# An attention kernel's second pair of heads: spread by transfers, rotated in one piece, with products of zeros behind two score chunks

## The chip, the cores and the metric

The kernel runs on one core of one Trainium2 chip. The metric is the device time of one execution in microseconds (us). Engines are named as the profile names them: PE (TensorE, matrix products and transposes), PEld (its weight loads), DVE (VectorE), ACT (ScalarE), POOL (GpSimd), and SP, the queue from which most transfers are issued.

## The reference

The program is an attention layer followed by two feed-forward layers, in float32. Attention has 4 batches of 8 heads, 576 positions and 64 columns per head:

```python
q_rot, k_rot = (rotate(q), rotate(k))     # rotary embedding, cos/sin by position
scores = scale * np.matmul(q_rot, k_rot.transpose(0, 1, 3, 2))
scores = scores - np.max(scores, axis=-1, keepdims=True)
attn = np.exp(scores)
attn = attn / (np.sum(attn, axis=-1, keepdims=True) + 1e-09)
return np.matmul(attn, v).astype(np.float32)
```

Its result, 2304 tokens of 512 columns, goes through `g = s * relu(x @ w_in)**2 + b; g @ w_out` (2048 hidden columns), and then through `silu(x @ w_gate) * (x @ w_val) @ w_out` with `silu` on the first factor (1536 hidden columns).

## The kernel before, in words

**Order of work.** The kernel is written as a list of operations (`op`, `sch.dma`), each with an engine, an estimated duration, a priority (lower goes first), dependences, and tokens for the buffers that it takes and gives back. A planner (`Schedule.run`, L63) plays the list through with these estimates: whenever an engine is free it takes the ready operation of lowest priority number that finds its buffers free, and emits its instructions. So the order on each engine and on the SP queue is fixed when the program is built. Only dependences of data are waited for on the chip. `o.next.append(x); x.need += 1` orders x behind the planned end of o without a wait on data. An operation that depends on one of its own engine becomes ready 0.06 us after the other's planned end; in that gap the planner gives the engine to whatever else is ready.

**Attention** works on 16 pairs of heads (two heads side by side in the 128 partitions). `prep(p)` (L448) loads a pair's queries and keys into `x` (two buffers), rotates them into `ry` (two buffers) in four steps, transposes `ry` on PE in three groups (L549, into the three PSUM banks `t`), and then spreads the transposed values, split into a high part and a rest for float32r products, into three arrays: `a` (queries, high and rest), `t` (keys, rest and high) and `kz` (keys, high, and zeros in the other rows). There are two sets of these, for even and odd pairs (z = 0, 1).

- Pair 0 rotates on DVE in three pieces. Pairs 1 and later rotate on POOL, each step one instruction over the whole pair: `y0` (L518), `y1` (L520), `y2` (L523), `y3` (L526). Pair 1 begins with a copy (L517) that waits for pair 0's rotation.
- Pairs 0 and 1 are spread by ACT and DVE (the `else` branch, L564 to L581): for each of three groups ACT writes `t`'s high part (L566), `a`'s high part (L566) and a copy of the first into `kz` (L568), and DVE writes the two rests (L571). Half of `kz` (64 partitions) was zeroed by POOL at the start (`zero`, L397).
- Pairs 2 and later: the layout of `ry` puts query and key columns alternately (L484), ACT writes one high part of all 128 rows into `qkhi` per group (`hi`, L556), DVE one rest into `qklo` (`lo`, L558), and five transfers on SP (`sp`, L586 to L598) copy every second row into `a`, `t` and `kz`. POOL zeroes `kz` whole ahead of that for pairs 2 and 3 (L585).

A pair's **values** are split on POOL in two instructions per head: `v0` (L611) and `v1` (L613), in `vh`.

`pair(p)` (L629) does nine score chunks of 128 queries (`s_mm`, L661, two PSUM buffers `s`), for each of them the row maximum on DVE (L664) and the exponential with its sum on ACT (L668). A chunk's PSUM buffer is free for the next chunk but one after its exponential. Of every three chunks, a `third` (L708) transposes the exponentials on PE (L724, L727), splits them on ACT (`ph`, L732) and DVE (`pl`, L739), multiplies them by the values (L754, L756) into the one bank `v`, and copies the result out on ACT (L767).

At the start PE runs 60 small products of zeros (`warm`, L435, L442) in the `v` bank.

```python
for i in range(WARM):
    op("pe", 0.11, warm, -100, (zeros[0][0],), (warm_tok,) if i == 0 else (), (warm_tok,))
```

The priorities that matter here: pair 0's and pair 1's `prep` have -390 and -290, pair 2's -40, pair 3's 60; pair 0's chunks run from 0 to 81, pair 1's from 100; the values of pair p, head j have 100p + 20j; the loads of values have 100p - 60 (pair 0 and 1: -200 and 40).

The feed-forward layers follow. Their weights are loaded and converted during the second half of attention, tied to score chunks of certain numbers.

Of the kernel before, what the change touches and what calls it, by code (L numbers as in the profile page):

```python
# [8 lines left out]
F32 = mybir.dt.float32  # L9
# [155 lines left out]
def t_pool(n):  # L165
    return 2.35e-3 * n + 0.08
# [11 lines left out]
def tile_attention_moe_moe(  # L178
# [34 lines left out]
    NE = 7  # L213
    LATE, LAST = 1 << 20, 1 << 21
    WARM = 60
    TP = 100
    PREP = 240
    TA = 50
# [178 lines left out]
    def zero(z, prio):  # L397
        o0 = op("pool", 0.2, lambda: nc.gpsimd.memset(a_t[z][:, S:S + 64].bitcast(F32), 0.0), prio)
        for x in (hi_t[z], lo_t[z]):
            gaps.append(op("pool", 0.2, lambda x=x: nc.gpsimd.memset(x[:, S:S + 64].bitcast(F32), 0.0), -250))  # L400
        o1 = op("pool", 1.0, lambda: nc.gpsimd.memset(kz_t[z][64:128].bitcast(F32), 0.0), prio)
        return (o0, o1)

    def load_x(p, g0, g1, prio, st, x_tok, after=()):
# [36 lines left out]
    for i in range(WARM):  # L441
        op("pe", 0.11, warm, -100, (zeros[0][0],), (warm_tok,) if i == 0 else (), (warm_tok,))  # L442

    first_rope = []

    qk_ops = list(sch.ops)

    def prep(p):  # L448
# [32 lines left out]

        def take_ry():
            st["ryt"] = rp_p.tile([128, PC, 2 * D], F32, tag="ry", name="ry")
            st["ry"] = st["ryt"].rearrange("p c (a d j) -> p j c a d" if p > 1 else "p c (j a d) -> p j c a d", j=2, a=2)  # L484

        def views2(a):
            return st["x"].rearrange("p j c (a d) -> p j c a d", a=2)[:, :, :, a], st["ry"][:, :, :, a]
# [4 lines left out]
        for g in range(G):  # L492
# [20 lines left out]
            if o is None and p:  # L513
                def y0():
                    take_ry()
                    if p == 1:
                        nc.gpsimd.tensor_copy(st["ryt"][:, 0, 0:1], first_rope[1]["ryt"][:, PC - 1, 2 * D - 1:2 * D])  # L517
                    nc.gpsimd.tensor_tensor(out=views2(0)[1], in0=views2(1)[0], in1=table(3, 1, 0, PC), op=ALU.mult)  # L518
                def y1():
                    nc.gpsimd.tensor_tensor(out=views2(1)[1], in0=views2(0)[0], in1=table(2, 1, 0, PC), op=ALU.mult)  # L520
                def y2():
                    xv = st["x"]
                    nc.gpsimd.tensor_tensor(out=xv, in0=xv, in1=table(0, 2, 0, PC), op=ALU.mult)  # L523
                def y3():
                    rv = st["ry"].rearrange("p j c a d -> p j c (a d)")
                    nc.gpsimd.tensor_tensor(out=rv, in0=st["x"], in1=rv, op=ALU.add)  # L526
                n2 = PC * D
                for y, fn in enumerate((y0, y1, y2, y3)):
                    o = op("pool", t_pool(n2 if y < 2 else 2 * n2), fn, pr, (o, *lds[0], *rt_op, *first_rope[:1]), (ry_tok,) if y == 0 else (), (x_tok,) if y == 3 else ())
                st["rope"] = o  # L530
            elif not p:
              o = None
              for y, fn in enumerate((r1, r0, r2, r3)):
                last = o if y else st.get("roped")
                deps = [*lds[g], (rt_ld[g], rt_op[2 * g], rt_op[2 * g + 1], None)[y]]
                o = op(eng, tt(fd if y > 1 else fd // 2), fn, pr + g, deps, (ry_tok,) if y == 0 and g == 0 else (),
                       (x_tok,) if y == 3 else (), port=eng == "dve")
                if last is not None:
                    last.next.append(o)
                    o.need += 1  # L540
              st["roped"] = o
              if g == G - 1:
                  first_rope.append(o)
                  first_rope.append(st)
# [3 lines left out]
                for c in range(PC // G):  # L548
                    nc.tensor.transpose(taken(ps)[:, :, c * 64:(c + 1) * 64], st["ryt"][:, g * (PC // G) + c], ident.rearrange("p (h r) -> p h r", h=2))  # L549
            hi_x, lo_x = hi_t[z], lo_t[z]  # L550
            acq = (ps_tok, hi_tok if p > 1 else tok) if g == 0 else (ps_tok,)
            prt = pr + 3 + g
            o = st["tr"] = op("pe", 0.33, tr, prt, (o, eye_op, st.get("tr"), *(zeros[z] if p < 2 else ())), acq, (ry_tok,))
            if p > 1:
                def hi(g=g):
                    nc.scalar.activation(out=place(hi_x, g), in_=taken(st["ps", g]), func=AF.Copy, scale=qs_t)  # L556
                def lo(g=g):
                    nc.vector.scalar_tensor_tensor(  # L558
                        out=place(lo_x, g), in0=taken(st["ps", g]), scalar=qs_t, in1=place(hi_x, g).bitcast(F32), op0=ALU.mult, op1=ALU.subtract
                    )  # L560
                o = st["hi0"] = op("act", t_act(CG, True, 1), hi, prt, (o, eye_op, st.get("hi0")))
                trs.append(op("dve", t_dve(CG, 2), lo, prt, (o,), (), (ps_tok,)))
            else:
                def act(dst, rows, g=g):  # L564
                    scale = D ** -0.5 if rows is up else 1.0
                    return lambda: nc.scalar.activation(out=place(dst, g), in_=taken(st["ps", g])[rows], func=AF.Copy, scale=scale)  # L566
                def again(dst, src, g=g):
                    return lambda: nc.scalar.activation(out=place(dst, g), in_=place(src, g).bitcast(F32), func=AF.Copy)  # L568
                def sub(dst, src, rows, g=g):
                    scale = D ** -0.5 if rows is up else 1.0  # L570
                    return lambda: nc.vector.scalar_tensor_tensor(  # L571
                        out=place(dst, g), in0=taken(st["ps", g])[rows], scalar=scale, in1=place(src, g).bitcast(F32), op0=ALU.mult, op1=ALU.subtract
                    )
                o1 = op("act", t_act(CG), act(t[dn], dn), prt, (o,))
                o2 = op("act", t_act(CG), act(a[up], up), prt, (o,))
                later = g if p == 0 else 0
                ops += [o1, op("dve", t_dve(CG), sub(t[up], t[dn], dn), prt, (o1,), (), (ps_tok,)),
                        op("act", t_act(CG, False), again(kz[up], t[dn]), prt, (o1,))]
                st.setdefault("a", []).append([o2, op("dve", t_dve(CG), sub(a[dn], a[up], up), prt + 3 * later, (o2,), (), (ps_tok,))])
                if p or g == 0:  # L580
                    ops += st["a"][-1]  # L581
        if p > 1:
            cleared = ()
            if p < 4:
                cleared = (op("pool", t_pool1(SP), lambda: nc.gpsimd.memset(kz.bitcast(F32), 0.0), pr + 6, trs[:1], (tok,)),)  # L585
            def sp(o, i, first=False):  # L586
                return sch.dma(
                    256 * SP, lambda: nc.sync.dma_start(out=o.bitcast(F32), in_=i.bitcast(F32)), pr + 6, (*trs, *cleared, *gaps),
                    (tok,) if first else (), (hi_tok,), pace=1.1
                )  # L590
            ev, od = slice(0, 128, 2), slice(1, 128, 2)
            ops = [
                sp(a[ev], hi_x[ev], p > 3),
                sp(a[od], lo_x[ev]),
                sp(t[ev], lo_x[od]),
                sp(t[od], hi_x[od]),
                sp(kz[ev], hi_x[od]),
            ]  # L598
            for o in ops[1:]:
                ops[0].next.append(o)  # L600
                o.need += 1
# [4 lines left out]
        for j in range(2):  # L606
            def part(j, h):
                return st["vh"][j][:, :, D * h:D * h + D]
            def v0(j=j):
                st["vh"][j] = v_p.tile([128, 5, 2 * D], F32R, tag="vh", name="vh")  # L610
                nc.gpsimd.tensor_scalar(out=part(j, 0), in0=st["vr"][:, j], scalar1=1.0, scalar2=0.0, op0=ALU.mult, op1=ALU.add)  # L611
            def v1(j=j):
                nc.gpsimd.tensor_tensor(out=part(j, 1), in0=st["vr"][:, j], in1=part(j, 0).bitcast(F32), op=ALU.subtract)  # L613
            vt = st["vh_tok"][j] = Token("vh")
            o = op("pool", t_pool1(320), v0, base + 20 * j, vls, (vt,))
            st["vh_op"][j] = op("pool", t_pool(320), v1, base + 20 * j, (o,), (), (tok_v,))
        return st

    turns, s_turns, v_turns = [], [], []

    def in_turn(o, turns=turns):
        if turns:
            turns[-1].next.append(o)
            o.need += 1
        turns.append(o)
# [3 lines left out]
    def pair(p, st):  # L629
# [10 lines left out]
        for u in range(NU):  # L640
# [32 lines left out]
                main = [*main, *st["a"][1 + u // 2]]  # L673
            o = s_prev = op("pe", t_mm(HS, 4 * len(terms)), s_mm, pr, (*main, s_prev), (s_tok, l_tok, *((sums[b]["tok"],) if pp == 0 else ())) if u == 0 else (s_tok,), (opb,))
            in_turn(o, s_turns)
            o = op("dve", t_dve(S), mx, pr, (o,))
            exps[u] = op("act", t_act(S, True, 1) + 0.09, ex, pr + 1, (o,), (e_tok[u],), (s_tok, l_tok))

# [280 lines left out]
        p, tag = (ps_t, "t") if tok.pool == "t" else (ps_v, "v")  # L959
        return p.tile([128, 512], F32, tag=tag, name="hb")[:, 0:n]  # L960

    sts, ends = {}, []
    for p in range(NP):
        sts[p] = prep(p)
    for p in range(NP):
        ends += pair(p, sts[p])
    n_att = len(sch.ops)
# [699 lines left out]
```

## Time and profile before

| | |
|---|---|
| median of 3 runs | 1093.91 us (1093.45 to 1094.46) |
| profiled execution | 1094.09 us, its span 1092.3 us |
| busy over the span | PE 1076.9, PEld 973.7, DVE 891.9, ACT 737.4, POOL 203.7 us |
| attention's score chunks | from 12.5 to 285 us |
| granted PE clock | 1.00 over the span |

The span is cut from the first to the last instruction of the profiled execution; the time of the execution is 1.8 us longer. Busy time is that of instructions at work; waits for semaphores and issuing of transfers don't count. A timeline row has the start, the duration and the operation; in brackets stands the idle time of the engine ahead of it, and what ended it.

### The profile page before, as it was taken

What the parts mean: (1) busy time and instruction counts of PE and PEld (TensorE: products, weight loads), DVE (VectorE), ACT (ScalarE), POOL (GpSimd) and SP (SyncE); (2) the same over time, 40 slices, a digit from 0 to 9 for tenths busy, and PEclk for the clock granted to TensorE, in tenths of its full rate; (3) what the DMA queues carried; (4) which work ended last, traced back from release to release, by engine and by line L of the source; (5) the groups of instructions that cost most, each with busy time, mean ns of one, the idle gap of its engine ahead of it and who ended that gap; (6) DMA issues with size and microseconds to landing.
All of it is one profiled execution on the core that took longest, in us unless ns stands there. A gap on an engine that the chain in (4) does not pass through costs nothing.

```text
span 1092.3 us, 17578 instructions
## 1 busy us (share of the span) xinstructions
PE 1076.9 (99%) x6188; PEld 973.7 (89%) x6188; DVE 891.9 (82%) x1575; ACT 737.4 (68%) x1511; POOL 203.7 (19%) x167
## 2 busy tenths in 40 slices
PE   8999999999999999999999999999999999999998
PEld 7899988888888799999888888999989999899996
DVE  6999999999988998879999998876596675976751
ACT  6998999999887776656665556655565554655550
POOL 7998878622210000000000000000000000000000
PEclk9999999999999999999999999999999999999999
DMA  4666867565569554482456654312231122311102
GB/s 124 205 201 218 272 215 246 144 227 181 141 221 259 156 173 164 141 237 87 167 184 204 227 173 140 132 56 70 88 96 39 58 68 78 96 50 44 54 1 57
DMA packets 111192, 155.51 MB, mean 142 GB/s; under 512 B 34416, under 2 KB 67200, under 8 KB 111104
## 3 DMA queue, kind: packets, MB, share of 16 engines
q1 hardware_dynamic: 110288, 153.60, 45.1%
q8 instruction: 49, 0.80, 0.3%
q10 hardware_dynamic: 816, 0.79, 0.2%
q14 instruction: 39, 0.32, 0.1%
HBM read 99.98 MB, written 32.58 MB: 121 GB/s over the span
## 4 chain that ended last, share of the span: by engine, by line
PE 81%; DVE 10%; ACT 4%; DMA 2%; issue 2%; POOL 1%; SPq 0%; DVEq 0%; POOLq 0%; ACTq 0%
PE hb L858 14%; PE hb L860 14%; PE hb L859 14%; PE acc L859 5%; PE acc L860 5%; PE acc L858 5%; PE acc L1449 5%; PE acc L1450 5%; PE acc L1448 5%; PE ps_s L661 3%; DVE nm L664 3%; DVE pl L739 3%; PE ps_t L724 2%; PE ps_av L754 2%; PE ps_av L756 1%
## 5 line engine op out<-in xcount | busy, mean ns | idle before, releaser
L858 PE MATMUL hb<-w 128*128 128x384 f32 (+1 forms) x728 | 250.9, 345 | 0.0
L860 PE MATMUL hb<-w 128*128 128x384 f32 (+1 forms) x728 | 250.5, 344 | 0.0
L859 PE MATMUL hb<-w 128*128 128x384 f32 (+1 forms) x728 | 250.1, 344 | 0.0
L858 PEld LDWEIGHTS hb<-w 128*128 128x128 f32 x728 | 136.7, 188 | 9.1 <-ACT tmp L1251 0.6
L859 PEld LDWEIGHTS hb<-w 128*128 128x128 f32 x728 | 136.7, 188 | 7.4
L860 PEld LDWEIGHTS hb<-w 128*128 128x128 f32 x728 | 136.6, 188 | 4.6
L668 ACT ACTIVATE e<-ps_s,nm 128x576 f32<-128x576 f32 x144 | 107.1, 744 | 9.9 <-DVE nm L664 8.9
L732 ACT ACTIVATE ph<-ps_t 128x512 fp32r<-128x512 f32 x192 | 105.7, 569 | 10.4 <-PE ps_t L724 9.2
L664 DVE TENSOR_REDUCE nm<-ps_s 128x1 f32<-128x576 f32 x144 | 107.8, 751 | 5.4 <-PE ps_s L661 4.2
L859 PE MATMUL acc<-gl,w 128*128 128x512 f32 (+1 forms) x288 | 107.0, 371 | 0.6 <-DVE gl L919 0.6
L860 PE MATMUL acc<-gh,w 128*128 128x512 f32 (+1 forms) x288 | 106.8, 371 | 0.0
L858 PE MATMUL acc<-gh,w 128*128 128x512 f32 (+1 forms) x288 | 106.6, 370 | 0.0
L661 PE MATMUL ps_s<-t,a 128*128 128x288 f32 x320 | 99.9, 329 | 4.6 <-ACT e L668 4.5
L739 DVE TENSOR_TENSOR pl<-ps_t,ph 128x512 fp32r<-128x512 f32 x144 | 95.4, 683 | 3.2 <-ACT ph L732 2.5
L754 PE MATMUL ps_av<-ph,vh 128*128 128x384 f32 (+1 forms) x320 | 97.0, 331 | 0.6 <-DVE ph L739 0.5
L1509 ACT ACTIVATE tmp<-hb 128x384 f32<-128x384 f32 x144 | 70.4, 489 | 34.3 <-PE hb L860 32.8
L661 PE MATMUL ps_s<-kz,a 128*128 128x288 f32 x320 | 88.9, 294 | 0.0
L724 PE MATMUL ps_t<-ident,e 128*128 128x128 f32 x576 | 86.1, 274 | 1.9 <-DVE a L571 1.1
L724 PEld LDWEIGHTS ps_t<-ident,e 128*128 128x128 f32 x576 | 67.8, 140 | 10.3 <-issue 1.7
L1147 DVE TENSOR_TENSOR w<-sums,w 128x512 fp32r<-128x512 f32 x104 | 68.3, 686 | 7.7 <-ACT w L1145 7.5
L756 PE MATMUL ps_av<-pl,vh 128*64 128x384 f32 (+1 forms) x256 | 72.5, 295 | 0.0
L661 PEld LDWEIGHTS ps_s<-t,a 128*128 128x128 f32 x320 | 60.2, 188 | 10.4 <-ACT e L668 9.1
(136 smaller groups left out, 2415.8 us busy)
## 6 DMA issues: line engine op xcount, KB each, us to landing
raw<-gv SPq DMA_DIRECT2D x36, 512.0 KB, 3.7
raw<-in_moe_w_out_dram SPq DMA_DIRECT2D x28, 512.0 KB, 4.0
x_d<-xr SPq DMA_DIRECT2D x64, 144.0 KB, 2.9
raw<-in_moe_w_in_dram SPq DMA_DIRECT2D x16, 512.0 KB, 3.8
raw<-up SPq DMA_DIRECT2D x16, 512.0 KB, 5.3
raw<-in_moe_w_gate_dram SPq DMA_DIRECT2D x12, 512.0 KB, 4.5
raw<-in_moe_w_val_dram SPq DMA_DIRECT2D x12, 512.0 KB, 4.8
gv<-dec SPq DMA_DIRECT2D x24, 256.0 KB, 2.5
```

What stands on the lines that cost most here:

```text
L661: nc.tensor.matmul(ps[:, hf * 512:hf * 512 + HS], a[:, q0:q0 + 128], m[:, k0:k0 + HS], start=y == 0, stop=y == len(todo) - 1)
L664: nc.vector.tensor_reduce(out=st["nm"][:, u:u + 1], in_=st["s", u], axis=AX.XY, op=ALU.max, negate=True)
L668: nc.scalar.activation(out=st["e", u].rearrange("p (f n) -> p f n", f=2), in_=st["s", u], func=AF.Exp, bias=st["nm"][:, u:u + 1], accum_ou ...
L724: nc.tensor.transpose(ps[:, z * 128:z * 128 + 128], st["e", u][:, kc * 128:kc * 128 + 128], ident)
L732: nc.scalar.activation(out=st["ph", y][0:rows, 512 * i:512 * i + n], in_=st["pt", y, i][0:rows, 0:n], func=AF.Copy)
L739: nc.vector.tensor_tensor(out=dst, in0=st["pt", y, i][0:rows, 0:n], in1=st["ph", y][0:rows, c].bitcast(F32), op=ALU.subtract)
L754: nc.tensor.matmul(ps, vv, st["ph", y][:, c], start=kc == 0, stop=kc == 4, skip_group_check=True)
L756: nc.tensor.matmul(ps[0:64], vv[:, 0:64], st["pl", y][:, c], start=False, stop=False, skip_group_check=True)
L858: nc.tensor.matmul(o, lh, rh, start=first, stop=False, skip_group_check=more)
L859: nc.tensor.matmul(o, lh, rl, start=False, stop=False, skip_group_check=more)
L860: nc.tensor.matmul(o, ll, rh, start=False, stop=last, skip_group_check=more)
L1509: nc.scalar.activation(out=st[key, f], in_=ps[name], func=AF.Copy)
```

## The change

1. Pair 1 is prepared as pairs 2 and later are: alternate layout of `ry`, `hi` and `lo` into the second set of `qkhi` and `qklo`, five transfers on SP. `kz` of the second set is zeroed whole at the start (128 partitions for 64); the zeroing for pair 3 goes, that for pair 2 stays.
2. The first steps of the values of pairs 0 and 1 are ordered behind pair 1's rotation on POOL, and pair 2's first rotation step behind the first head's values of pair 0. So nothing comes between pair 1's four steps.
3. Sixteen more products of zeros (two instructions each) stand on PE: eight ordered behind pair 0's second score chunk, eight behind its fourth.

```diff
+    FILL = 8
...
-        o1 = op("pool", 1.0, lambda: nc.gpsimd.memset(kz_t[z][64:128].bitcast(F32), 0.0), prio)
+        o1 = op("pool", 1.0, lambda: nc.gpsimd.memset((kz_t[z] if z else kz_t[z][64:128]).bitcast(F32), 0.0), prio)
...
+    fill = [op("pe", 0.13, warm, -150, (), (), (warm_tok,)) for _ in range(2 * FILL)]
+
-    first_rope = []
+    first_rope, behind_rope, sts = [], [], {}
...
-            st["ry"] = st["ryt"].rearrange("p c (a d j) -> p j c a d" if p > 1 else "p c (j a d) -> p j c a d", j=2, a=2)
+            st["ry"] = st["ryt"].rearrange("p c (a d j) -> p j c a d" if p else "p c (j a d) -> p j c a d", j=2, a=2)
...
                     o = op("pool", t_pool(n2 if y < 2 else 2 * n2), fn, pr, (o, *lds[0], *rt_op, *first_rope[:1]), (ry_tok,) if y == 0 else (), (x_tok,) if y == 3 else ())
+                    if p == 2 and y == 0:
+                        sts[0]["vh_op"][0].next.append(o)
+                        o.need += 1
...
-            acq = (ps_tok, hi_tok if p > 1 else tok) if g == 0 else (ps_tok,)
+            acq = (ps_tok, hi_tok if p else tok) if g == 0 else (ps_tok,)
...
-            if p > 1:
+            if p:
                 def hi(g=g):
...
-        if p > 1:
-            cleared = ()
-            if p < 4:
+        if p:
+            cleared = (zeros[1][1],) if p == 1 else ()
+            if p == 2:
...
-                sp(a[ev], hi_x[ev], p > 3),
+                sp(a[ev], hi_x[ev], p != 2),
...
             st["vh_op"][j] = op("pool", t_pool(320), v1, base + 20 * j, (o,), (), (tok_v,))
+            if p < 2:
+                behind_rope.append(o)
...
             in_turn(o, s_turns)
+            if p == 0 and u in (1, 3):
+                for x in fill[u // 2 * FILL:u // 2 * FILL + FILL]:
+                    o.next.append(x)
+                    x.need += 1
...
+    for o in behind_rope:
+        sts[1]["rope"].next.append(o)
+        o.need += 1
```

## Rows read from the trace of the kernel before

**Rows 1.** Busy time by stretch: length, PE, PEld, DVE, ACT, POOL, clock, DMA, GB/s.
```profile
14.00:28.00 14.00, 9.65 (x65) 8.01 (x66) 10.32 (x17) 11.42 (x27) 14.00 (x9) 1.00 0.24 72
...
42.00:140.00 98.00, 97.86 (x774) 91.70 (x773) 90.38 (x147) 90.09 (x215) 84.52 (x61) 1.00 0.73 230
140.00:300.00 160.00, 155.32 (x1155) 138.65 (x1154) 155.34 (x253) 148.88 (x347) 78.72 (x69) 1.00 0.61 191
```

**Rows 2.** PE's timeline, 15 to 47 us: start, duration, operation, idle before.
```profile
15.19 0.40 PE L661 MATMUL ps_s<-t,a 128*128 128x288 f32 x1 [1.19 <-ACT e L668]
...
17.69 0.40 PE L661 MATMUL ps_s<-t,a 128*128 128x288 f32 x1 [0.99 <-ACT e L668]
...
21.50 0.34 PE L754 MATMUL ps_av<-ph,vh 128*128 128x384 f32 x1
...
26.41 0.63 PE L724 MATMUL ps_t<-ident,e 128*128 128x128 f32 x4 [1.08 <-DVE a L571]
27.86 0.40 PE L661 MATMUL ps_s<-t,a 128*128 128x288 f32 x1 [0.82 <-ACT e L668]
...
28.85 0.38 PE L661 MATMUL ps_s<-t,a 128*128 128x288 f32 x1
...
30.09 0.45 PE L754 MATMUL ps_av<-ph,vh 128*128 128x384 f32 x1 [0.47 <-DVE ph L739]
...
46.73 0.38 PE L661 MATMUL ps_s<-t,a 128*128 128x288 f32 x1
```

**Rows 3.** Busy time in PE's four idle times from 24.58 to 30.09.
```profile
sum 2.63, PE 0.01 PEld 0.07 DVE 2.36 ACT 2.56 POOL 2.63; mean PE 0.00 PEld 0.02 DVE 0.59 ACT 0.64 POOL 0.66
```

**Rows 4.** ACT's timeline, 19 to 34 us.
```profile
19.50 0.60 ACT L732 ACTIVATE ph<-ps_t 128x512 fp32r<-128x512 f32 x1 [1.13 <-PE ps_t L724]
...
26.97 0.74 ACT L668 ACTIVATE e<-ps_s,nm 128x576 f32<-128x576 f32 x1
...
28.42 1.44 ACT L732 ACTIVATE ph<-ps_t 64x384 fp32r<-64x384 f32 x3
...
32.79 1.05 ACT L556 ACTIVATE qkhi<-pst,ident 128x384 fp32r<-128x384 f32 x2
```

**Rows 5.** POOL's timeline, 10 to 29 us.
```profile
10.29 1.40 POOL L518 TENSOR_TENSOR ry<-x,rt 128x576 f32<-128x576 f32 x1
11.86 0.46 POOL L611 TENSOR_SCALAR vh<-vr 128x320 fp32r<-128x320 f32 x1 [0.17 <-DMA vr<-in_v_dram]
...
13.66 0.87 POOL L613 TENSOR_TENSOR vh<-vr,vh 128x320 fp32r<-128x320 f32 x1
...
17.08 1.41 POOL L518 TENSOR_TENSOR ry<-x,rt 128x576 f32<-128x576 f32 x1
18.45 2.66 POOL L526 TENSOR_TENSOR ry<-x,ry 128x1152 f32<-128x1152 f32 x1
...
26.30 2.69 POOL L526 TENSOR_TENSOR ry<-x,ry 128x1152 f32<-128x1152 f32 x1
```

**Rows 6.** SP's timeline around 37 us, and landing times of L588's transfers to 140 us.
```profile
36.26 0.51 SPq L588 DMA_DIRECT2D a<-qklo  x1
...
38.16 0.69 SPq L588 DMA_DIRECT2D kz<-qkhi  x1
...
DMA to landing us min/median/max: 2.5/3.5/5.8
```

**Rows 7.** Spreading copies by line, ACT and DVE: count, busy us, mean ns.
```profile
L568 ACT ACTIVATE kz<-t 64x384 fp32r<-64x384 f32 x3 | 1.5, 514 | 0.0
L566 ACT ACTIVATE t<-pst 64x384 fp32r<-64x384 f32 x3 | 1.5, 487 | 0.1
...
L556 ACT ACTIVATE qkhi<-pst,ident 128x384 fp32r<-128x384 f32 x3 | 1.6, 575 | 0.0
...
L558 DVE SCALAR_TENSOR_TENSOR qklo<-pst,ident,qkhi 128x384 fp32r<-128x384 f32 x3 | 1.7, 609 | 0.0
```

**Rows 8.** PE's timeline at 9 us, products of zeros.
```profile
9.26 1.50 PE L439 MATMUL warm<-a 128*64 128x64 f32 x22
```

More of the change, by code (lines that the diff above doesn't have):

```diff
@@ L960, in get_hb @@
         return p.tile([128, 512], F32, tag=tag, name="hb")[:, 0:n]
-    sts, ends = {}, []
+    ends = []
     for p in range(NP):
         sts[p] = prep(p)
+    for o in behind_rope:
+        sts[1]["rope"].next.append(o)
+        o.need += 1
     for p in range(NP):
```

## The prediction

> **What bounds the kernel now.** I first read the busy time by stretches of the start. From 42 us to 140 us TensorE is busy 97.86 of 98 us, and from 140 to 300 us it is busy 155.32 of 160 us with VectorE just as full (155.34) [rows 1]. So from 42 us on attention runs at TensorE's pace, and a microsecond gained ahead of 42 us should be carried along; lost time is found only before. From 14 to 28 us TensorE is busy 9.65 of 14 us [rows 1], and that is where the change works.
>
> Next I read TensorE's timeline there, looking at idle times and what ended them. Two waits, of 1.19 and 0.99 us, stand ahead of the third and the fifth score chunk, each for the exponentials of two chunks before [rows 2]: there are two score banks, and nothing else is ready. These come from the loop product, maximum, exponential. A second group lies around 25 to 30 us: waits for the second pair's `a` on VectorE, for an exponential (the first pair's last chunk, 27.86), for `ph` (30.09) [rows 2]. With a shorter fourth one ahead of them they make 2.63 us, in which ScalarE is busy 2.56 [rows 3]. ScalarE is the cause: between 22.5 and 27 us it does the nine copies that spread the second pair's queries and keys, and the seventh exponential, which the score bank waits for, starts only behind them at 26.97 [rows 4].
>
> **The change, part by part.** Sums are made against the profiled execution (1094.09 us; span 1092.30). It stands 0.18 us above the median of 1093.91, so a gain found there is taken off the median.
>
> *Rotation in one piece.* On GpSimd the second pair's four rotation steps begin at 10.29, with two steps of values and one multiplication of the third pair between them; the last begins at 18.45 and takes 2.66 us [rows 5], so it ends at 21.1. In one piece it is two of 1.40 and two of 2.66 (the third taken like the last): 10.29 + 8.12 = 18.4, 2.7 us sooner. Behind it stand the first pair's values, 0.46 and 0.87 [rows 5], with the second head's 0.46 between: ready at 20.2, where the first product with values ran at 21.50 [rows 2]. Cost nothing; without that margin of 1.3 us the product waits. The third pair's rotation, whose last step began at 26.30 [rows 5], has the same work ahead, but two more foreign pieces can slip into its gaps (0.46 and 0.87, or twice 1.41): 1.3 to 2.8 us later. Its copies landed by about 38.16 + 3.5 = 41.7 [rows 6], its first chunk ran at 46.73 [rows 2]: margin 5.0 us, of which the delay (2.8) and the gain (2.2) together take 5.0 at the far end. Cost nothing, but thin there.
>
> *Spread by transfers.* ScalarE loses nine copies of 0.487 to 0.514 (the third group, of `a`, taken like that of `t`), 4.5 us, and gains three of 0.575, 1.7 us [rows 7]: 2.8 us less ahead of the seventh exponential. VectorE does three of 0.609 [rows 7] for six; I put that into no sum. As the rotation ends sooner, the three can begin in ScalarE's idle 1.13 us that ends at 19.50 [rows 4]. So the exponentials that TensorE waits for at 27.86 come some 3 us sooner, and the whole 2.63 us [rows 3] has no cause left.
>
> The new wait is that of the second pair's first chunk, at 28.85 before [rows 2], for the five transfers. The third pair shows the price: from its first `qkhi` at 32.79 to the issue of its last transfer at 38.16 are 5.4 us with foreign work between, and landing takes 3.5 (2.5 to 5.8) [rows 4, 6]. At its pace, from 19.5: 28.4. Back to back: three of 0.575, one of 0.609, 1.9 from the second issue to the fifth (36.26 to 38.16), 3.5 to land, 7.7 in all [rows 6, 7]: 27.2. Wanted it is at 28.85 - 2.63 = 26.2. So it is 1.0 to 2.2 us late. Behind it in TensorE's order wait its own products only; the first pair's transposes and value products of its second and third part cover it (they are what TensorE did at 30.09 and after, and ScalarE has them fed until about 32, see the rival below). I let a part of it show: 0.4 us, between 0 (cover complete) and 2.2 (none), nearest to 0 since ScalarE and VectorE have cover work throughout.
>
> The Trainium skill ("DMA: Bandwidth & Descriptors", Anatomy of one DMA) gives a transfer a fixed 2.0 us plus its bytes over the bandwidth; by that, as an estimate, 304 KB would land in 2.7 us where the row has 3.5, and the wait would be 0.8 us shorter. The row decides.
>
> *Products of zeros.* Twice eight. Before, 22 records, two to a product, take 1.50 us [rows 8], so eight take 1.1. They run in the 1.19 and 0.99 us that TensorE spends waiting for the exponentials: the first eight fit, the second reach 0.1 us over. An idle time is counted from the modelled end of a product, behind the point where the next could have started, so I take 0, with 0.2 as the other end; without those waits it would be 2.2. What they give: the granted clock from 14 to 28 us is 1.00 without them, the upper of its two levels (2.4 GHz), through all the waits [rows 1]. Nothing is to be regained: 0. The Trainium skill ("TensorE: Matmul & The Clock Gate", HAM oscillation) holds that idle gaps throw the clock back to half rate; in this stretch no record shows it, and where it did happen the products would be worth up to the busy time at double. By the page the products matter, by the row they don't.
>
> *The rest.* Zeroing the second pair's `kz` whole instead of half costs GpSimd nothing that shows (as many columns, and done long before use), and one later zeroing goes, on an engine that TensorE doesn't wait for after 42 us. Five more issues on SP stand ahead of loads that aren't due soon: 0. As the planner sets all orders anew, work after 30 us will stand in another order: I bound that by 1.5 us to either side, about a third of the 4.7 us that TensorE is idle from 140 to 300 us [rows 1].
>
> Sum: -2.63 + 0.4 = -2.2 us, to 1094.09 - 2.2 = 1091.9 for that execution, 1091.7 against the median. 0.2% is 2.2 us, about what a measurement of this kernel can tell from no change: the forecast lies on that border.
>
> **The rivals.**
>
> *More than the stall goes.* With ScalarE some 3 us ahead nothing of the new wait shows, and part of the 4.7 us after 140 goes too: -2.63 - 1.5 = -4.1 at the far end, -3.4 in the middle, 1090.5. For it: VectorE has less to do as well. Against: after 140 us VectorE binds, and its work there isn't touched.
>
> *The gain is given back.* TensorE, earlier by 2 us, meets VectorE full from 140 us on or the third pair's late rotation, and waits there: -0.3, 1093.6. For it: 155.34 of 160 busy [rows 1], and the thin margin of 5.0 us. Against: weight loads are tied to score chunks and shift with them.
>
> *Slower: the transfers come behind others on SP.* SP issues in order. If the third pair's five value loads and the fourth pair's two come ahead of the five spreads, at up to 0.69 each [rows 6], 4.8 us, and landing takes 5.8, the last lands at 28.4 + 4.8 + 2.3 = 35.5. ScalarE runs out of first-pair work at 19.5 + five exponentials of 0.74, twelve splits and three evictions of 0.48 (1.44 for three), three of 0.575 [rows 4, 7] = 32.1, and TensorE with it. It then idles 3.4 us and runs the slow loop of 1.19 and 0.99 [rows 2] for the second pair too: 5.6 - 2.63 = +3.0, 1096.9. It decides from a landing at 32.5 on. Against it: the plan gives the spreads precedence over value loads.
>
> *The page's rule.* If TensorE, waiting for the transfers, fell to half its clock, the second pair's first 2 us of products would take 4: a loss of 2 us more than the forecast, 1093.7, without the products of zeros reaching it. No row bears it out: from 14 to 28 us TensorE was idle 4.35 us and the clock stayed at 1.00 [rows 1].
>
> **How the numbers follow.** Forecast 0.46 (own range 1090.7 to 1092.7, just half of it beyond the border), more than the stall 0.20, given back 0.18, slower 0.13, the clock 0.03. Faster by over 0.2%: 0.24 + 0.20 = 0.44; within: 0.22 + 0.18 + 0.03 = 0.43; slower 0.13. The range runs from the second case's far end with some of the reorder (1089.3) to 1095.4, which takes in the given-back case with 1.5 us of reorder and leaves out most of the slower one: 0.13 above, some 0.05 below.
>
> **What would show it.** Right: the rotation ends by 18.5; three `qkhi` of 0.575 by 21.5; the seventh exponential at about 24; TensorE idle between 19 and 31 us under 0.8; `kz` landing 27 to 28.5; a second-pair first chunk at 27 to 29; granted clock 1.00; TensorE's stretch from 42 on as full as before. Wrong: an idle time of over 1 us that a transfer ends ahead of the second or third pair's first chunk; third or fifth chunk later than 15.3 or 17.8 (products of zeros in the way); gains of 2 us at 42 us that are gone at 300.

## The result, and the profile after

The changed kernel takes 1102.78 us (median of 6 runs, 1099.87 to 1104.53), where the kernel before took 1093.68 (6 runs beside it, 1091.83 to 1095.43): ratio 1.008, interval 1.0067 to 1.0093. It is 9.1 us slower; the forecast was 2.2 us faster, with 1095.4 as the upper end. Its profiled execution is the fastest of the six (1099.87 us, span 1098.1), 5.8 us longer than that of before.

The start went much as forecast. PE's timeline of the changed kernel, 15 to 31 us, answers to [rows 2]; L669 is the score product, L766 the product with values:

```profile
15.21 0.40 PE L669 MATMUL ps_s<-t,a 128*128 128x288 f32 x1
...
17.74 0.40 PE L669 MATMUL ps_s<-t,a 128*128 128x288 f32 x1
...
20.53 0.34 PE L766 MATMUL ps_av<-ph,vh 128*128 128x384 f32 x1
...
29.19 0.66 PE L736 MATMUL ps_t<-ident,e 128*128 128x128 f32 x4 [0.85 <-DVE pl L751]
...
31.04 0.38 PE L669 MATMUL ps_s<-t,a 128*128 128x288 f32 x1
```

Third and fifth chunk come at 15.21 and 17.74, behind the products of zeros and no later than before by more than 0.05 us. Of the 2.63 us of idle time [rows 3] one of 0.85 is left. ACT's timeline, to [rows 4]:

```profile
20.04 0.58 ACT L562 ACTIVATE qkhi<-pst,ident 128x384 fp32r<-128x384 f32 x1
...
21.22 1.06 ACT L562 ACTIVATE qkhi<-pst,ident 128x384 fp32r<-128x384 f32 x2
...
23.88 0.73 ACT L676 ACTIVATE e<-ps_s,nm 128x576 f32<-128x576 f32 x1
```

Three copies instead of nine; the seventh exponential starts at 23.88, where it was 26.97. So TensorE gets ahead. To follow that, I count the products of `a` with `t` in PE's timeline (20 to a pair, 320 in all) and compare the starts of the same one. The 41st, the third pair's first, starts at 45.06 instead of 46.73: **1.67 us ahead**. The 311th, in the last pair, starts at 283.82 instead of 277.72: **6.10 us behind**. The loss lies between. PE's timeline of the changed kernel at these two:

```profile
45.06 0.40 PE L669 MATMUL ps_s<-t,a 128*128 128x288 f32 x1
...
283.82 0.29 PE L669 MATMUL ps_s<-t,a 128*128 128x288 f32 x1
```

and of before at the 311th (its 41st is the last line of [rows 2]):

```profile
277.72 0.30 PE L661 MATMUL ps_s<-t,a 128*128 128x288 f32 x1
```

Busy time by stretch, columns as in [rows 1], which the first three lines answer to:

```profile
14.00:28.00 14.00, 13.64 (x112) 11.65 (x112) 10.65 (x17) 10.87 (x27) 13.92 (x11) 1.00 0.46 156
...
42.00:140.00 98.00, 95.64 (x756) 89.39 (x755) 91.38 (x143) 89.15 (x213) 83.75 (x61) 1.00 0.73 234
140.00:300.00 160.00, 151.95 (x1138) 136.88 (x1138) 154.85 (x250) 144.20 (x337) 74.28 (x67) 0.99 0.59 183
...
156.00:164.00 8.00, 6.96 (x43) 6.70 (x44) 6.57 (x12) 4.71 (x12) 2.02 (x3) 0.79 0.46 125
```

TensorE is idle 2.4 us from 42 to 140 us (before 0.1) and 8.0 us from 140 to 300 (4.7), and from 156 to 164 us its granted clock is 0.79 on average: a part of it ran at the lower level, 1.2 GHz. PE's timeline shows three long waits there:

```profile
91.33 0.29 PE L702 MATMUL psr<-ident,l 128*36 128x128 f32 x1 [1.67 <-DVE l L698]
...
157.04 0.36 PE L766 MATMUL ps_av<-ph,vh 128*128 128x192 f32 x1 [2.00 <-DVE ph L751]
...
209.39 0.66 PE L736 MATMUL ps_t<-ident,e 128*128 128x128 f32 x4 [2.40 <-DVE pl L751]
```

Each is released by VectorE. VectorE's timeline at these places:

```profile
88.26 2.61 DVE L695 TENSOR_SCALAR l<-l 128x36 f32<-128x36 f32 x1
...
152.86 3.26 DVE L329 SCALAR_TENSOR_TENSOR dec<-raw,dec 128x512 uint32<-128x512 uint32 x1
...
205.74 2.99 DVE L329 SCALAR_TENSOR_TENSOR dec<-raw,dec 128x512 uint32<-128x512 uint32 x1
```

and GpSimd's:

```profile
88.15 2.68 POOL L529 TENSOR_TENSOR ry<-x,ry 128x1152 f32<-128x1152 f32 x1
...
152.86 2.70 POOL L529 TENSOR_TENSOR ry<-x,ry 128x1152 f32<-128x1152 f32 x1
...
205.55 2.64 POOL L526 TENSOR_TENSOR x<-x,rt 128x1152 f32<-128x1152 f32 x1
```

The first is an addition to 36 columns (the row sums, L695), 0.17 us where nothing is in its way; the other two are a step of weight decoding (L329), 0.68 us elsewhere. They are 2.44, 2.58 and 2.31 us too long, and each ends 0.04, 0.56 and 0.54 us behind the end of a rotation step of GpSimd (L526, L529) that began at most 0.2 us ahead of it or with it. In the trace of before the same addition and the rotation step next to it stand in the other order, by 0.22 us. VectorE's timeline of before:

```profile
91.12 0.31 DVE L683 TENSOR_SCALAR l<-l 128x36 f32<-128x36 f32 x1
```

and GpSimd's:

```profile
91.34 2.71 POOL L526 TENSOR_TENSOR ry<-x,ry 128x1152 f32<-128x1152 f32 x1
```

**Theory P**: VectorE instructions on operands in SBUF wait for the end of a GpSimd instruction that has begun, and the new plan's order makes three of them meet the longest ones. **Theory O**: the new order makes TensorE wait for its data, whatever GpSimd does. **Theory S**: the second pair's transfers and its late first chunk (31.04) cost it. Beside them stood the question of what the products of zeros do.

### The profile page after: what moved, and what is told of

Its sections match the earlier page's. It is cut to its first block, busy times and chain, and to the rows that moved or that the text cites. A ratio compares the mean times of both kernels' runs of the same rounds, so it can differ in the third digit from the quotient of the medians.

```text
span 1098.1 us, 17625 instructions
## 1 busy us (share of the span) xinstructions
PE 1078.4 (98%) x6220; PEld 976.3 (89%) x6220; DVE 896.7 (82%) x1572; ACT 734.6 (67%) x1505; POOL 200.1 (18%) x166
## 4 chain that ended last, share of the span: by engine, by line
PE 79%; DVE 11%; ACT 4%; DMA 2%; issue 1%; POOL 1%; SPq 1%; ACTq 0%; DVEq 0%
PE hb L870 14%; PE hb L872 14%; PE hb L871 14%; PE acc L871 5%; PE acc L872 5%; PE acc L870 5%; PE acc L1464 5%; PE acc L1465 5%; PE acc L1463 5%; DVE nm L672 3%; DVE pl L751 3%; PE ps_s L669 3%; ACT e L676 2%; PE ps_t L736 2%; PE ps_av L766 1%
## 5 line engine op out<-in xcount | busy, mean ns | idle before, releaser
L669 PE MATMUL ps_s<-t,a 128*128 128x288 f32 x320 | 99.5, 328 | 2.1 <-ACT e L676 1.2
L766 PE MATMUL ps_av<-ph,vh 128*128 128x384 f32 (+1 forms) x320 | 97.8, 333 | 2.6 <-DVE ph L751 2.0
L669 PE MATMUL ps_s<-kz,a 128*128 128x288 f32 x320 | 88.9, 294 | 0.0
L1556 ACT ACTIVATE tmp<-tmp 128x384 f32<-128x384 f32 x72 | 37.7, 523 | 43.7 <-DVE tmp L1529 43.5
```

Source lines behind the costliest of these rows:

```text
L669: nc.tensor.matmul(ps[:, hf * 512:hf * 512 + HS], a[:, q0:q0 + 128], m[:, k0:k0 + HS], start=y == 0, stop=y == len(todo) - 1)
L766: nc.tensor.matmul(ps, vv, st["ph", y][:, c], start=kc == 0, stop=kc == 4, skip_group_check=True)
```

## The experiments

All ratios are to the kernel before, run on the same chip. Its medians there were 1093.68 beside the changed kernel, 1093.57 beside e1 to e4, 1093.63 beside e5 to e9, 1092.91 beside e10 and e11, 1093.11 beside e12 and e13; kernels of different groups are compared by their distance to it. In the table, the start of the k-th product of `a` with `t` against before (us; negative is earlier), each from its one profiled execution:

| kernel | 41st | 91st | 101st | 171st | 231st | 311th | median us, ratio (interval) |
|---|---|---|---|---|---|---|---|
| changed | -1.67 | -0.67 | 1.53 | 5.86 | 5.09 | 6.10 | 1102.78, 1.008 (1.0067 to 1.0093) |
| e1_halves | -1.62 | -0.65 | -0.29 | 2.35 | 0.19 | 1.20 | 1098.19, 1.004 (1.0028 to 1.0052) |
| e2_quarters | -1.69 | -0.27 | 3.43 | 5.18 | 3.30 | 4.34 | 1104.45, 1.010 (1.0081 to 1.0119) |
| e3_no_zeros | -0.64 | 0.34 | 4.12 | 6.93 | 6.12 | 7.13 | 1103.29, 1.0086 (1.0071 to 1.01) |
| e4_zeros_only | 0.51 | 0.51 | 0.50 | 1.66 | 1.13 | 1.11 | 1092.44, 0.9992 (0.9983 to 1.0) |
| e5_one_piece | 2.41 | 3.03 | 3.14 | 4.52 | 3.98 | 1.77 | 1098.85, 1.0049 (1.0031 to 1.0066) |
| e6_transfers | 1.79 | 0.88 | 1.01 | 5.31 | 6.08 | 6.70 | 1103.29, 1.0089 (1.0074 to 1.0105) |
| e8_short | -1.70 | -0.72 | -0.35 | 0.21 | -2.57 | -1.52 | 1094.13, 1.0007 (0.9997 to 1.0017) |
| e9_before_short | 0.37 | 0.36 | 0.34 | 0.23 | -0.28 | -0.29 | 1092.25, 0.9995 (0.9983 to 1.0007) |
| e10_ordered | -1.71 | -0.73 | -0.35 | 0.51 | -2.34 | -1.02 | 1095.78, 1.0027 (1.0016 to 1.0038) |
| e11_before_zeros_ordered | -0.01 | -0.02 | -0.05 | -0.10 | -0.57 | -0.51 | 1092.19, 0.9988 (0.9979 to 0.9997) |
| e12_gh_first | -1.65 | -0.70 | -0.36 | 0.16 | -2.98 | -1.75 | 1093.72, 0.9998 (0.9988 to 1.0008) |
| e13_before_zeros_gh | -0.10 | -0.18 | -0.18 | -0.12 | -0.66 | -0.71 | 1092.29, 0.999 (0.9978 to 1.0001) |

**Shorter GpSimd instructions, same orders.** In the changed kernel, for pairs 2 and later, each long step becomes two instructions; in e2_quarters it becomes four (`pieces(4)`), and each short step two. The third step:

```diff
-                    xv = st["x"]
-                    nc.gpsimd.tensor_tensor(out=xv, in0=xv, in1=table(0, 2, 0, PC), op=ALU.mult)
+                    for c0, c1 in pieces(2):
+                        xv = st["x"][:, :, c0:c1]
+                        nc.gpsimd.tensor_tensor(out=xv, in0=xv, in1=table(0, 2, c0, c1), op=ALU.mult)
```

> The changed kernel with the third and fourth rotation step of pairs 2 and later issued as two GpSimd instructions each (1.3 us for 2.65), in the same planned order on every engine. Theory P (the time is lost where VectorE instructions wait for a GpSimd instruction to end: 2.44, 2.58 and 2.31 us too long at 88, 153 and 206 us in the changed kernel's trace): none of them is more than 1.4 us too long, and the time falls by 2 to 6 us against the changed kernel, to 1097 to 1101. Theory O (the new order itself makes TensorE wait for its data): within 1 us of the changed kernel, 1102 to 1104.

> As the halves, with four GpSimd instructions for each of the two long steps and two for each of the two short ones (0.7 us each). Theory P: no VectorE instruction over 0.8 us too long before 290 us, TensorE idle from 42 to 300 us down from 10.4 us to about 5, no fall of the granted clock at 157 us, 1092 to 1095, lower than with halves. Theory O: 1102 to 1104.

Halves: 1098.19, 4.6 us above before where the changed kernel is 9.1 above, as P expected. The addition at 88 us now began 0.3 us ahead of GpSimd's first half and took 0.39 us; the decoding step at 152 us waited for one half. VectorE's timeline of e1 there:

```profile
151.89 1.87 DVE L329 SCALAR_TENSOR_TENSOR dec<-raw,dec 128x512 uint32<-128x512 uint32 x1
```

and GpSimd's, two instructions in one row:

```profile
151.90 3.28 POOL L537 TENSOR_TENSOR ry<-x,ry 128x512 f32<-128x512 f32 x2
```

Quarters went against what P as I had put it expected: 1104.45. The addition took 4.10 us. VectorE's timeline of e2 at 88 us:

```profile
88.67 4.10 DVE L703 TENSOR_SCALAR l<-l 128x36 f32<-128x36 f32 x1
```

and GpSimd's, with the number of instructions at the end of a row:

```profile
87.73 1.57 POOL L529 TENSOR_TENSOR ry<-x,rt 128x256 f32<-128x256 f32 x2
89.26 3.04 POOL L533 TENSOR_TENSOR x<-x,rt 128x256 f32<-128x256 f32 x4
92.27 0.46 POOL L625 TENSOR_SCALAR vh<-vr 128x320 fp32r<-128x320 f32 x1
```

It came in while the second of six short instructions standing in a row (two of one step, four of the next) was at work. The last of them ended at 92.30, the value split behind them (L625) at 92.73, and the addition 0.04 us later, as at 88 us in the changed kernel (90.83 and 90.87). So it lasted over six GpSimd instructions, not one, and cutting them up is no sure remedy. Why VectorE did get its turn between the two halves I can't say. The trace is that of the fastest execution of e2 (1100.13 us); what the others, up to 1107.12, lose besides is not on record.

**The long steps taken away.** In the changed kernel and, as the control, in the one before, the third and fourth rotation step of pairs 2 and later are done for one of nine column blocks. The third step:

```diff
-                    xv = st["x"]
-                    nc.gpsimd.tensor_tensor(out=xv, in0=xv, in1=table(0, 2, 0, PC), op=ALU.mult)
+                    n = PC if p < 2 else 1
+                    xv = st["x"][:, :, 0:n]
+                    nc.gpsimd.tensor_tensor(out=xv, in0=xv, in1=table(0, 2, 0, n), op=ALU.mult)
```

> The changed kernel with the third and fourth rotation step of pairs 2 and later done for one of nine column blocks only (GpSimd instructions of about 0.4 us for 2.65; queries and keys of these pairs are left mostly unrotated). Every engine keeps its order. Theory P (VectorE waits for long GpSimd instructions): the three long waits at 88, 153 and 206 us are gone, the lead of the second and third pair (1.7 us at the 41st score product) is kept to 140 us and beyond, 1091 to 1095. Theory O (the new order starves TensorE by its data): 1100 to 1104, with the same idle times of TensorE at 91, 157 and 209 us.

> The kernel before with the same shortening (the same steps left out), as the control. Its trace has no such wait over 0.6 us before 290 us, so by theory P it gains little: 1092 to 1094, and the changed kernel with short steps is 0 to 2 us faster than it. If shorter GpSimd steps help by themselves, it falls by as much as the changed kernel does (6 us or more).

Measured 1094.13 and 1092.25. Without long steps the changed kernel, all its orders kept, is 0.5 us above before instead of 9.1; the same shortening puts the kernel before 1.4 us below itself by the medians, 0.5 by the ratio. The last pair is now reached 1.52 us ahead of before. On the way the lead is lost (0.35 us at the 101st product, 0.21 behind at the 171st) and won again (2.57 ahead at the 231st); I leave that open. Theory O is out. P's second half, that the shortened changed kernel beats the shortened one before, didn't come true: it is 1.9 us slower. Something behind attention takes some 3 us back.

**One part alone.** The kernel before with the ordering on GpSimd alone (e5), with the transfers alone (e6, the changed kernel less the two orderings and the zeros):

```diff
+                    if p == 2 and y == 0:
+                        sts[0]["vh_op"][0].next.append(o)
+                        o.need += 1
...
+            if p < 2:
+                behind_rope.append(o)
```

> The kernel before with the rotation of the second pair in one piece alone (values and third pair ordered behind it). The second pair still spreads by ScalarE and VectorE. Gain in the start by the earlier rotation alone: 0 to 1 us at the 41st score product, as ScalarE's nine copies remain. Theory P: what comes after depends on whether VectorE instructions meet a long GpSimd step; each meeting over 2 us costs 1.5 to 3 us, so 1092.5 with none and 1096 or more with two. Theory S (the transfers and their late first chunk cause the loss): 1092 to 1094.

> The kernel before with the spread by transfers alone: rotation interrupted as before, no products of zeros. The second pair's first chunk is later than the changed kernel's 31.0, at 33 to 34, as its rotation ends 2.7 us later; lead at the 41st score product 0 or a loss of 1 us. Theory S: as slow as the changed kernel, 1100 or more, with the loss at the second and third pair. Theory P: the loss, if any, lies after 80 us where VectorE meets long GpSimd steps, and the time is 1093 to 1095 if it meets none.

Both are slow, 1098.85 and 1103.29, by 5.2 and 9.7 us. e6 is late at its start, by more than expected (1.79 us at the 41st), is 1.0 us behind at the 101st, meets the same decoding step twice (3.26 us at 152, 2.98 at 205), and ends up where the changed kernel does. S doesn't hold: the second pair comes 2.7 us later than in the changed kernel, and the time is the same. e5 doesn't have the transfers at all. It loses 2.4 us at the start, where its clock is 0.76 (below), and at 141 us VectorE's last step of a loaded tile of tokens takes 2.66 us for 0.68. VectorE's timeline of e5:

```profile
141.61 2.66 DVE L852 TENSOR_TENSOR x<-xs,x 128x512 fp32r<-128x512 f32 x1
```

and GpSimd's:

```profile
141.59 1.31 POOL L843 TENSOR_TENSOR xs<-x 128x512 f32<-128x512 f32 x1
142.84 0.89 POOL L616 TENSOR_TENSOR vh<-vr,vh 128x320 fp32r<-128x320 f32 x1
```

Again it waits for two GpSimd instructions in a row. So such a meeting is no part of the change in itself: each new plan draws the meetings anew. It is not what makes e5 slow, though: e5 is 1.77 us behind at the 311th product, so some 3.4 of its 5.2 us are lost behind attention, which I did not follow.

**The meetings prevented.** The whole changed kernel, plus one-column copies that make GpSimd wait: where the plan puts a rotation step behind such a VectorE instruction, GpSimd first reads a column of its result.

```diff
+    def behind_dve():
+        if sch.mark is not None and sch.now - sch.mark_t < 6:
+            nc.gpsimd.tensor_copy(scr, sch.mark)
+        sch.mark = None
...
             def r0():
+                sch.mark = sums[b]["l"][:, 0:1]
...
                 def y3():
+                    behind_dve()
```

> The changed kernel, whole, with seven one-column copies on GpSimd: a rotation step that the plan puts behind a VectorE instruction on two SBUF operands (row sums, weight decoding) first reads a column of its result, so GpSimd can't begin the step while that instruction still waits to start. All orders stay. Theory P: the waits of 2.4, 2.6 and 2.3 us at 88, 153 and 206 us fall under 0.8, TensorE's idle of 1.7, 2.0 and 2.4 us behind them goes, attention's last chunks come at 276 to 278 us as with the shortened steps (276.2), and the time is 1093 to 1096. Theory O: 1100 to 1104.

> The kernel before with the sixteen products of zeros and the same copies on GpSimd; no other part of the change. Its VectorE instructions meet no rotation step for over 0.6 us, so by theory P the copies give at most 0.5 us: 1091.5 to 1093, as with the products of zeros alone (1092.4). If the copies help by something else, it falls by as much as the changed kernel does with them.

1095.78: 2.9 us above before where the changed kernel is 9.1 above, so some 6 us less, with the same work in the same orders and seven small copies more. In the profiles the 311th product comes 7.1 us sooner. VectorE's timeline of e10 at 88 us:

```profile
88.23 0.17 DVE L716 TENSOR_SCALAR l<-l 128x36 f32<-128x36 f32 x1
```

and GpSimd's:

```profile
87.28 0.87 POOL L639 TENSOR_TENSOR vh<-vr,vh 128x320 fp32r<-128x320 f32 x1
88.95 0.18 POOL L464 COPY scr<-l 128x1 f32<-128x1 f32 x1 [0.80 <-DVE l L720]
89.09 2.71 POOL L549 TENSOR_TENSOR ry<-x,ry 128x1152 f32<-128x1152 f32 x1
```

The copy (L464) waits 0.80 us for the row sums, the step starts 0.94 later than in the changed kernel, nobody waits for it, and the addition takes 0.17. No VectorE instruction is over 0.6 us too long before 300 us, and the clock is 1.00 in every stretch. This shows P for attention. In the kernel before, which has no such wait over 0.6 us ahead of 290 us, the copies change nothing: ratio 0.9988, beside 0.9992 with the zeros alone.

**The rest.** e10 reaches the last pair 1.02 us ahead of before and is 2.9 us slower. In its ACT timeline, in the first feed-forward layer:

```profile
354.56 0.82 ACT L946 ACTIVATE r<-r,bv,sv 128x512 f32<-128x512 f32 x1
358.17 0.66 ACT L329 ACTIVATE dec<-raw 128x512 f32<-128x512 f32 x1 [2.79 <-DMA up<-dec]
358.73 0.61 ACT L949 ACTIVATE gh<-r 128x512 fp32r<-128x512 f32 x1
```

A decode (L329) that waits 2.79 us for its weights stands ahead of `gh` (L949), which could start at 355.4 and which TensorE waits for. PE's timeline of e10:

```profile
359.39 0.50 PE L893 MATMUL acc<-gh,w 128*128 128x512 f32 x1 [1.02 <-ACT gh L949]
```

In e1, e3 and e6 TensorE's wait for `gh` is 1.78, 1.33 and 1.37 us, and behind it, within 363 to 372 us, the granted clock falls to 0.50 for a while; in e2 and e8 (1.41 and 1.60) it does not fall. In the changed kernel's own profile, its fastest execution, the decode waits 1.63 us and TensorE not for `gh`, so how much of its 9.1 us lies here is not shown. The next edit plans `gh` ahead of the decode, by its priority (`ew - 200`); with `lag` it is ready at the planned end of the operation that it depends on, so nothing slips in between:

```diff
-                o = op("act", t_act(n, False, 2), whole, ew, (o,))
-            o1 = op("act", t_act(n, False, 0 if sq_eng == "act" else 1), gh, ew, (o,))
+                o = op("act", t_act(n, False, 2), whole, ew, (o,), lag=-0.06)
+            o1 = op("act", t_act(n, False, 0 if sq_eng == "act" else 1), gh, ew - 200, (o,))
```

> The changed kernel with the copies on GpSimd, and in the first feed-forward layer the high parts of the activations (gh) planned ahead of weight decoding on ScalarE; attention keeps its order. The changed kernel with the copies ends attention 1.0 us ahead of before (276.7 against 277.7 for the 311th score product) but its time is 2.9 us behind. Theory F (the rest is lost in the first feed-forward layer, where gh stands on ScalarE behind a decode that waits 2.8 us for its load): the idle of 1.0 us at 359 us goes and the time falls by 1 to 2 us, to 1094 to 1095. If the rest lies elsewhere: 1095.3 to 1096.3, as without the edit.

> The kernel before with the products of zeros, the copies on GpSimd and the same order of gh: a candidate that should beat both kernels. TensorE's idle of 1.28 and 0.44 us at 485 and 488 us in the version without this order has another cause (VectorE's gl), so theory F expects little here: 1091.5 to 1092.5.

ACT's timeline of e12 at the same place:

```profile
353.85 0.80 ACT L946 ACTIVATE r<-r,bv,sv 128x512 f32<-128x512 f32 x1
354.69 0.63 ACT L949 ACTIVATE gh<-r 128x512 fp32r<-128x512 f32 x1
357.23 0.67 ACT L329 ACTIVATE dec<-raw 128x512 f32<-128x512 f32 x1 [1.90 <-DMA up<-dec]
```

1093.72, 0.6 us above before where e10 is 2.9 above: some 2 us less, and the change with both repairs is level with before (0.9998). Its profiled execution is the fastest of its twelve (1092.09) and keeps to its end the 1.75 us that it has ahead at the end of attention, in spite of one more wait of TensorE, 1.65 us at 385 us, for ScalarE; the median shows no gain, and where the other executions lose it is not on record. e13 came out as expected, and no better than e11. It has the zeros, the copies and the order of `gh` as e12 has them, but not the transfers and the rotation in one piece, and it ran on the same chip: 1092.29 against 1093.72 for e12. So even repaired, these two parts show no gain; if anything they cost 1.4 us (the intervals of the two ratios overlap).

**The products of zeros.** The changed kernel without them, and before with nothing else:

```diff
-    FILL = 8
+    FILL = 0
```

> The changed kernel without the sixteen products of zeros; all other instructions stand in the same order. If they neither cost nor give (prediction): granted clock 1.00 until 42 us, chunk starts within 0.1 us up to 42 us, time within 1.5 us of the changed kernel. If they hold the clock up: granted clock under 1.00 between 14 and 28 us and a later start of the second pair, 1 us or more slower.

> The kernel before with the sixteen products of zeros alone. Prediction: within 0.5 us of before (1093.7), third and fifth chunk within 0.1 us of 15.19 and 17.69. If they were in the way or upset the order: 1 us or more slower, with waits of VectorE for GpSimd as in the changed kernel.

Both times agree with "neither cost nor give" to within their noise (1103.29 against 1102.78; 1092.44, ratio 0.9992 up to 1.0). The clock doesn't. Busy time by stretch of e3 (no zeros):

```profile
14.00:28.00 14.00, 11.81 (x72) 10.56 (x73) 9.86 (x16) 10.00 (x24) 13.92 (x11) 0.88 0.48 161
```

of e5 (no zeros):

```profile
14.00:28.00 14.00, 9.55 (x48) 8.24 (x47) 8.26 (x13) 9.32 (x21) 13.92 (x11) 0.76 0.33 89
```

and of e4 (zeros), the stretch behind it:

```profile
28.00:42.00 14.00, 14.00 (x104) 13.51 (x104) 12.74 (x22) 13.10 (x32) 14.00 (x11) 0.88 0.60 192
```

Without the zeros the clock fell in the first pair in the profiles of e3, e5 and e6 (0.88, 0.76, 0.88 from 14 to 28 us), and e3 is 1.0 us less ahead at the 41st product than the changed kernel. With zeros and transfers it was 1.00 to 42 us in all profiles (changed, e1, e2, e8, e10, e12). In e4, which keeps the 2.63 us of idle [rows 3], it fell behind that, as it did in e9, which has the same start without the zeros (0.88 from 28 to 42 us); in e11 and e13, with the zeros and that start, it did not. The kernel before is at 1.00 in the profile shown, while over its runs the mean clock of the span lies between 0.994 and 1.0. In 30 of its 80 executions beside the experiments it is 0.996 or less, and these take 0.9 to 2.2 us longer than the others of their chip (medians); none of the 33 executions of e4, e11 and e13 is under 0.997. Where in the span before's clock fell in those 30 no trace shows.

**The lowest ratio** is that of e11, which is before with zeros and copies: 1092.19, 0.9988 (0.9979 to 0.9997), 1.3 us below before. It is the best of three such kernels, and the intervals of the other two (e4, e13) reach 1. e4 has nearly all of it, so it is the zeros' doing, as far as it can be told from noise.

## Why the prediction was wrong

- **Rotation in one piece: right.** Its last step began at 15.88 and took 2.69 us, ending at 18.6 (forecast 18.4); the first product with values ran at 20.53, 0.3 us after they were ready: the margin of 1.3 was used to the most part and cost nothing. The third pair's rotation ended at 31.9, 2.9 us later than before, just past the far end of the forecast (2.8), and was not waited for.
- **Spread by transfers: right in the main term.** ScalarE's relief is as forecast, the seventh exponential 0.1 us from the 24 named. The second pair's first chunk came at 31.04, 2 us later than the range named for it, without an idle time ahead of it: the plan had put it there, behind first-pair work that covered it. The last transfer went out at 26.58 and landed 3.5 us later, at 30.1, where 27 to 28.5 was named, but still in time. The 2.7 us that the prediction set beside the row, from the Trainium skill ("DMA: Bandwidth & Descriptors", Anatomy of one DMA), would not have fitted: that section is on transfers issued by GpSimd, while these go out on SP, and in this trace the second pair's took 3.2 to 3.6 us. The residue was 0.85 us of idle instead of 0.4. The lead at the 41st product, 1.67 us, is the forecast 2.2 less 0.5.
- **Products of zeros: placed right, their worth wrong.** They cost nothing. That they give nothing rested on the clock of one execution of before. In kernels without them it did fall to the lower level behind the idle times of this stretch (0.76 and 0.88 from 14 to 28 us in e5, e3 and e6, 0.88 from 28 to 42 us in e9), so the section of the Trainium skill that I had set aside ("TensorE: Matmul & The Clock Gate", HAM oscillation) has the trace on its side here; the size is about 1 us (1.03 us at the 41st product, changed against e3; ratios 0.9988 to 0.9992 for before).
- **The step that failed** is this one: "As the planner sets all orders anew, work after 30 us will stand in another order: I bound that by 1.5 us to either side, about a third of the 4.7 us that TensorE is idle from 140 to 300 us". An idle time of before bounds what can be won back, not what a new order can lose. The sign that the prediction named for it came: 1.67 us ahead at 45 us, 6.10 us behind at 284. Measured, the distance to before falls from 9.1 us to 2.9 without the meetings of VectorE and GpSimd (e10), and to 0.6 with `gh` ahead of the decode as well (e12): some 6 us and some 2, by medians whose noise is about 1 us. With that the change is level with before, and not the 2.2 us ahead that were forecast. So a second step failed too: "a microsecond gained ahead of 42 us should be carried along". The gain is there (1.65 us at the 41st product of e12), but the medians don't have it at the end; that part stays open.
- **The rival "the gain is given back"** had VectorE full from 140 us on as its mechanism, and the loss did come by way of VectorE. But its price, a gain that is used up, was wrong in kind: with VectorE at 155.34 of 160 us [rows 1], each wait of 2.3 to 2.6 us reached TensorE for the most part (1.67, 2.00 and 2.40 us), and behind the second one the clock was lower for a while on top. **The slower rival** (transfers behind others on SP) didn't occur: one value load of 0.64 us stood between.
- **What could have been read.** The code has it: the planner keeps operations marked `port` on VectorE away from GpSimd in its own times (L96). And the page "GPSIMD Engine Reference" of the Trainium skill (Specifications) says that GpSimd shares its SBUF interfaces with VectorE, with contention for VectorE instructions in a two-port mode or with two SBUF inputs. The trace agrees, and adds the price: the addition in place, the decoding with two operands in SBUF and the rest of loaded tokens were held up for up to 3.9 us; row maxima and the rests `pl`, which read PSUM, never were, nor was the reciprocal of the row sums, which does work in SBUF (0.38 us at 88.72 in e1, beside a half of a rotation step). In the rows of before, 91.12 and 91.34 stood 0.22 us apart: a plan that holds two engines apart by estimated times, which they don't keep on the chip, is safe only by such margins.

## What to carry to other kernels

Where an order is planned from estimated durations, an edit at the start is also a new draw for everything behind it: price it by the resources that the plan only keeps apart on paper, and look how narrowly the present order misses them. Here a GpSimd step of 2.7 us acted as a lock for some VectorE instructions on SBUF operands (2.3 to 2.6 us too long); if the order between two such instructions matters, make it a dependence (one-column reads were enough here: some 6 us), and give it to the engine that has time. One profile's granted clock says little about a stretch with idle times; look at several executions.

## What was unexpected of the hardware

VectorE's wait isn't bounded by the GpSimd instruction at work: six short ones in a row kept it out for 3.9 us (e2), two others in a row for 2.0 (e5); in e1 it got in between two. So it did in before: the addition that began at 91.12, while a value split ran until 91.38, took only 0.31 us, though the rotation step followed at 91.34. When it does is left open. A 2.0 us wait of TensorE at 157 us, behind other work at the full clock, was followed by some microseconds at the lower one (0.79 on average over 8 us): 4.3 us were lost between the 151st and the 171st product (1.58 to 5.86), where e10, without the meeting, lost 0.7 (0.23 ahead to 0.51 behind). The 2.40 us wait at 209 us was not followed by a fall (1.00 from 209 to 212 us).
